# Window attention with its backward pass: the x loads of the loop issued by GpSimd in place of SyncE

## The chip, the cores and the metric

The kernel runs on one core of one Trainium2 chip. A core has a matrix engine (TensorE, PE in the profile; its weight loads are listed apart as PEld), a vector engine (VectorE, DVE), a scalar engine (ScalarE, ACT), GpSimd (POOL) and SyncE (SP). They run side by side, each with its own stream of instructions, and wait for each other on semaphores. Data moves between main memory (HBM) and the on-chip memory (SBUF) by transfers that sixteen DMA engines carry out; an engine only issues them. In this kernel SyncE and GpSimd issue nearly all of them. Matrix products land in PSUM, eight banks that VectorE and ScalarE read out.

The metric is the device time in microseconds (us). The kernel before takes 2007.22 us, the median of three runs (1998.82, 2007.22 and 2007.71).

## What is computed

The operation is attention inside windows of 8 by 8 tokens over an image of 256 by 256 tokens with 384 channels, with one head, and its backward pass:

```python
qkv = xw @ wqkv                        # xw: (1024 windows, 64 tokens, 384)
q, k, v = qkv[..., :C], qkv[..., C:2*C], qkv[..., 2*C:]
p = softmax(einsum('bqc,bkc->bqk', q, k) * C ** -0.5)
o = einsum('bqk,bkc->bqc', p, v) @ wo  # out_0, after the windows are put back
# and from grad_out: the gradients of x (out_1), wqkv (out_2) and wo (out_3)
```

All inputs and outputs are bfloat16. `x`, `grad_out`, `out_0` and `out_1` are 50 MB each, so about 102 MB are read from HBM and 102 MB written.

## The kernel before

**Tiling.** A tile holds two windows, that is 128 tokens on 128 partitions. A "quad" is four such tiles, eight windows one below the other, and there are 128 quads. For a quad the kernel holds `xq` (128 tokens by 4 tiles by 384 channels of x), `dq` (the same of `grad_out`), and their transposes `xT` and `dT` with the channels on the partitions. The weights are folded ahead of the loop into four 384 by 384 matrices (`A_sb`, `AT_sb`, `B_sb`, `BT_sb`, lines 84 to 102).

**The software pipeline.** The order of the work is written out by hand: `tc.manual_schedule` (line 359) covers all five engines, so that each engine executes its instructions in the order in which the Python code emits them. One call of `step(c, b, a, ahead)` (lines 315 to 351) works on four quads at once. In step i, quad i+1 is in stage A (its products with `BT_sb` and `A_sb`, function `project`, give `yz`), quad i in stage B (scores `sd`, softmax, the products `uq` and `vq`), quad i-1 in stage C (`attend`, which makes the rows of `out_0` and `out_1`), and quad i+3 is loaded. In between, `filler` (lines 307 to 313) puts pieces of the weight gradient of three finished quads, `gf_group`, into the stream of TensorE: one piece ahead of each half of `attend`, six pieces for three quads.

**The transfers of a step, in the order of each queue.** SyncE issues for step i:

1. `load_turn` (lines 121 to 129): the transposes `dT` and `xT` of quad i+2. They are DMA transposes from SBUF to SBUF.
2. `turn` (line 231): the transpose `PS` of quad i's probabilities and score gradients, which needs the last operation of the softmax (`soft` step 5, line 219).
3. `load` (lines 114 to 119): four loads of `x` for quad i+3.
4. `to_tokens` (line 165): the transpose `tok` of quad i+1's `yz`, which needs the evictions of both projections (lines 161 and 163).

GpSimd issues for step i four loads of `grad_out` for quad i+3 (line 119), then the stores of `attend` for quad i-1: twelve in all, six after each pair of tiles (lines 287 to 292). The stores read from buffers `ob`, eight for each of `o` and `d`.

A queue waits in order: while its next transfer waits for data or for a buffer, those behind it wait too. TensorE reads `dT` in stage A of the next step, `xT` shortly after it, `PS` in stage C of the next step.

**Buffers.** `xq` has 2 * GQ + 4 = 10 buffers, because the weight gradient still reads a quad's `xq` some steps after `attend`. `dq` has 6, `xT` and `tok` 3, `dT`, `yz` and `PS` 2.

**Ahead of the loop** (lines 360 to 363) the first three quads are loaded and two of them transposed.

Of the kernel before, what the change touches and what calls it, by code (L numbers as in the profile page):

```python
# [22 lines left out]
def kernel(  # L23
# [21 lines left out]
    nc = tc.nc  # L45
# [61 lines left out]
    def windows(ap, st, first, count=2):  # L107
        row, col = st["at"]
        return ap[0, row + WIN * first:row + WIN * (first + count), col:col + WIN, :]
# [1 line left out]
    LO, HI = slice(0, WT), slice(WT, P)  # L111
    OTHER = {0: HI, WT: LO}

    def load(st):
        st["xq"] = xq = grp.tile([P, QUAD, C], BF16, tag="xq", name="xq", bufs=2 * GQ + 4)
        st["dq"] = dq = qp.tile([P, QUAD, C], BF16, tag="dq", name="dq", bufs=6)
        for t in range(QUAD):
            nc.sync.dma_start(out=xq[:, t, :], in_=windows(x, st, 2 * t))
            nc.gpsimd.dma_start(out=dq[:, t, :], in_=windows(grad_out, st, 2 * t))  # L119

    def load_turn(st):
        xq, dq = st["xq"], st["dq"]
        st["xT"] = xT = qp.tile([P, QUAD, CK, P], BF16, tag="xT", name="xT", bufs=3)
        st["dT"] = dT = qp.tile([P, QUAD, CK, P], BF16, tag="dT", name="dT")
        for src, dst in ((dq, dT), (xq, xT)):
            k = G_ON_PE if src is dq else 0
            if k < QUAD:
                nc.sync.dma_start_transpose(out=dst[:, k:].rearrange("p t m k -> p (t m) k"),
                                            in_=src[:, k:].rearrange("p t c -> p (t c)"))
# [49 lines left out]
    def over_k(ap, n=P):  # L179
        return ap.unsqueeze(2).broadcast_to([n, QUAD, WT])  # L180

    def soft(st, step):
        sd = st["sd"]
        if step == 0:
# [111 lines left out]
    def gf_group(sts):  # L296
        n = len(sts) * QUAD
        for f in range(2):
            for ma in range(CK):
                pw = ring.tile([P, C], F32, tag="r", name="pg")  # L300
                for i in range(n):
                    st, t = sts[i // QUAD], i % QUAD
                    product(pw[:], st["xq"][:, t, ma * P:(ma + 1) * P], st["UW"[f] + "q"][:, t, :], i == 0, i == n - 1)
                nc.vector.tensor_tensor(out=GF_acc[:, f, ma, :], in0=pw[:], in1=GF_acc[:, f, ma, :], op=ALU.add)  # L304
                yield

    def filler(n):
        while n and fill:
            try:
                next(fill[0])  # L310
                n -= 1
            except StopIteration:
                fill.pop(0)

    def step(c, b, a, ahead):


        def on(st):
            return (lambda f, *r: f(st, *r)) if st is not None else (lambda f, *r: None)
        C_, B, A = on(c), on(b), on(a)  # L320
        B(scores)
        B(soft, 0)
        B(uv, 0, 0)
        B(uv, 0, 1)
        B(soft, 1)
        B(uv, 1, 0)
        B(uv, 1, 1)
        B(soft, 2)
        B(soft, 3)
        B(uv, 2, 0)  # L330
        B(uv, 2, 1)
        for t in range(QUAD):
            A(grad_turn, t)
        B(uv, 3, 0)
        B(uv, 3, 1)
        B(soft, 4)
        for mo in range(CK):
            A(project, 0, mo)
        B(soft, 5)
        B(turn)  # L340
        if ahead is not None:
            load(ahead)
        filler(1)
        C_(attend, (0, 1))
        split[0] = True
        for mo in range(CK):
            A(project, 1, mo)
        A(to_tokens)
        filler(1)
        split[0] = ALL  # L350
        C_(attend, (2, 3))
# [4 lines left out]
    sts = [{"at": q, "i": i} for i, q in enumerate(quads)]  # L356
    n = len(sts)
    AHEAD = 3
    with tc.manual_schedule(engines=MANUAL):
        for i in range(min(AHEAD, n)):  # L360
            load(sts[i])
            if i < AHEAD - 1:
                load_turn(sts[i])
        held = []
        get = lambda i: sts[i] if 0 <= i < n else None
        for i in range(-1, n + 1):
            if AHEAD - 1 <= i + AHEAD - 1 < n:
                load_turn(sts[i + AHEAD - 1])
            step(get(i - 1), get(i), get(i + 1), get(i + AHEAD) if i >= 0 else None)
            if i > 0:  # L370
                held.append(sts[i - 1])
                sts[i - 1] = None
            if held and (len(held) == GQ or i == n):
                fill.append(gf_group(held))
                held = []
        split[0] = False
        filler(1 << 30)
# [62 lines left out]
```

## Time and profile before

| | |
|---|---|
| time, median of three runs | 2007.22 us |
| time of the profiled run | 1999.63 us |
| span of the profile | 1997.5 us |
| ScalarE busy | 1405.4 us (70%) |
| VectorE busy | 1317.2 us (66%) |
| GpSimd busy, nearly all of it issuing | 1122.9 us (56%) |
| moved by the DMA engines | 425.62 MB, mean 213 GB/s |
| loads of `x`: issuer, count, size, median time to landing | SyncE, 512, 96 KB, 4.0 us |
| loads of `grad_out` | GpSimd, 512, 96 KB, 3.9 us |
| transposes `dT`, `xT`, `tok`, `PS`: issuer, count of each, median time to landing | SyncE, 128, 6.4, 6.7, 8.4 and 4.6 us |

The first line of the page gives busy time, share of the span and number of instructions for each engine. SyncE is not in it, because an instruction that issues a transfer counts as busy on GpSimd alone; what SyncE does is read from the timeline of its queue (marked SPq). A line of the timeline has a start and a length in microseconds, the engine, the line of the kernel, the operation, the tile written and the tile read, the number of instructions merged into the line, and in brackets how long the engine stood idle before and what released it. "Landing" is the time from issue until the data is known to have arrived. A line of the waits reads "who waited <- for whom: us in total, times, longest".

### The profile page before, as it was taken

Reading aid. Unit: us, or ns where it says so; the run is one execution under the profiler, and the core shown is the slowest. Engines: PE = TensorE matmul, PEld = TensorE weight load, DVE = VectorE, ACT = ScalarE, POOL = GpSimd, SP = SyncE. Lnnn points to the kernel's source line nnn. Section 1 sums busy time; section 2 is a strip of 40 time slices with the busy share of each in tenths; the row PEclk is TensorE's granted clock in tenths of the full one; section 3 lists DMA queues with packets and bytes.
Section 4 is the critical chain, followed back from the end, with each engine's and each line's share of the span. In section 5 each row is a group of like instructions: output and inputs, shape, how many; then the busy total and the mean of one; then the engine's idle time right before and its main releaser. Section 6 shows DMA issues by size and latency. Waiting matters only on the chain. (4 is left out here: it accounts for less than half of the span.)

```text
span 1997.5 us, 52374 instructions
## 1 busy us (share of the span) xinstructions
PE 1967.7 (99%) x19418; PEld 1192.8 (60%) x19418; DVE 1317.2 (66%) x2979; ACT 1405.4 (70%) x3213; POOL 1122.9 (56%) x2054
## 2 busy tenths in 40 slices
PE   8899999999999999999999999999999999999998
PEld 4456656665666666566566656666665566566655
DVE  5666666666666666666666666666666666666666
ACT  5776767677777767777776777677776777776773
POOL 3555555565555556555655555565555556555643
PEclk9999999999999999999999999999999999999999
DMA  9999999999999999999999999999999999999993
GB/s 201 211 217 223 208 213 215 224 215 221 216 218 223 210 213 223 219 219 208 227 210 223 219 211 213 223 223 215 215 214 214 212 217 213 223 211 222 217 206 96
DMA packets 1042272, 425.62 MB, mean 213 GB/s; under 512 B 925792, under 2 KB 1016672, under 8 KB 1042016
## 3 DMA queue, kind: packets, MB, share of 16 engines
q1 hardware_dynamic: 943312, 270.60, 81.2%
q0 software_dynamic: 98304, 151.39, 31.1%
q8 instruction: 152, 2.49, 0.6%
q14 instruction: 104, 0.85, 0.1%
q10 hardware_dynamic: 400, 0.29, 0.0%
HBM read 101.84 MB, written 101.84 MB: 102 GB/s over the span
## 5 line engine op out<-in xcount | busy, mean ns | idle before, releaser
L292 POOL DMA_DIRECT2D out_dram<-o x256 | 139.2, 544 | 707.4 <-ACT o L264 697.4
L264 ACT CAST o<-po 128x384 bf16<-128x384 f32 x512 | 220.4, 482 | 370.0 <-PE pu L253 355.2
L304 DVE TENSOR_TENSOR GF_acc<-pg,GF_acc 128x384 f32<-128x384 f32 x258 | 144.0, 558 | 495.0 <-PE pg L145 343.8
L147 PEld LDWEIGHTS <-xT 128*128 128x128 bf16 x3072 | 291.8, 98 | 182.1
L147 PE MATMUL pj<-B_sb,xT 128*128 128x384 bf16 x1536 | 333.4, 326 | 0.0
L147 PE MATMUL pj<-AT_sb,xT 128*128 128x384 bf16 x1536 | 333.3, 326 | 0.0
L119 POOL DMA_DIRECT2D dq<-in_grad_out_dram x512 | 274.1, 547 | 66.0 <-DMA out_dram<-o 37.7
L147 PE MATMUL pj<-dT,BT_sb 128*128 128x512 bf16 x1152 | 269.7, 379 | 8.8 <-DMA dT<-dq 7.3
L145 PE MATMUL pj<-xT,A_sb 128*64 128x512 bf16 x2304 | 273.0, 380 | 1.6 <-DMA xT<-xq 1.6
L229 ACT CAST uq<-pj 128x384 bf16<-128x384 f32 x512 | 247.6, 484 | 30.6 <-PE pj L147 27.1
L229 ACT CAST vq<-pj 128x384 bf16<-128x384 f32 x512 | 249.9, 488 | 2.4 <-ACT uq L229 0.3
L145 PEld LDWEIGHTS <-xq 128*64 128x64 bf16 x3000 | 210.6, 110 | 46.3
L264 ACT CAST d<-pd 128x384 bf16<-128x384 f32 x512 | 225.2, 503 | 0.4 <-ACT o L264 0.2
L147 PEld LDWEIGHTS <-xq 128*128 128x128 bf16 x1572 | 153.6, 98 | 114.9 <-issue 0.3
L207 ACT COPY ps<-Pb 64x256 bf16<-64x256 bf16 x256 | 103.3, 403 | 149.6 <-DVE Pb L204 148.1
L163 ACT CAST yz<-pj 128x512 bf16<-128x512 f32 x384 | 206.3, 630 | 2.1 <-PE pj L145 1.8
L161 ACT CAST yz<-pj 128x512 bf16<-128x512 f32 x384 | 206.4, 639 | 1.1 <-ACT vq L229 0.7
L145 PEld LDWEIGHTS <-A_sb 128*64 128x64 bf16 x2304 | 155.7, 109 | 84.9 <-DMA xT<-xq 2.0
L147 PEld LDWEIGHTS <-BT_sb 128*128 128x128 bf16 x1152 | 111.5, 98 | 133.9 <-DMA dT<-dq 13.6
L147 PE MATMUL pg<-Uq,xq 128*128 128x384 bf16 x1032 | 181.6, 326 | 0.0
L258 PE MATMUL pd<-tok,ps 128*64 128x384 bf16 x1024 | 181.2, 344 | 0.0
L253 PE MATMUL pu<-xq,PS 64*64 64x384 bf16 x1024 | 174.9, 335 | 4.5 <-DMA PS<-ps 4.3
(67 smaller groups left out, 3382.2 us busy)
## 6 DMA issues: line engine op xcount, KB each, us to landing
xq<-in_x_dram SPq DMA_DIRECT2D x512, 96.0 KB, 4.0
dq<-in_grad_out_dram POOLq DMA_DIRECT2D x512, 96.0 KB, 3.9
out_dram<-o POOLq DMA_DIRECT2D x256, 96.0 KB, 4.2
out_dram<-o POOLq DMA_DIRECT2D x512, 48.0 KB, 4.4
out_dram<-d POOLq DMA_DIRECT2D x256, 96.0 KB, 4.4
out_dram<-d POOLq DMA_DIRECT2D x512, 48.0 KB, 4.4
dT<-dq SPq DMA_TRANSPOSE x128, 6.4
xT<-xq SPq DMA_TRANSPOSE x128, 6.7
```

Of the source, the lines that this page charges most:

```text
L119: nc.gpsimd.dma_start(out=dq[:, t, :], in_=windows(grad_out, st, 2 * t))
L145: nc.tensor.matmul(out[h], lhsT=lhsT[:, h], rhs=rhs, start=start, stop=stop)
L147: nc.tensor.matmul(out, lhsT=lhsT, rhs=rhs, start=start, stop=stop)
L161: ENG[EV["z"][mo]](out=yz[:, mo, :, 0:4:3, :], in_=pj[:])
L163: ENG[EV["y"][mo]](out=yz[:, mo, :, 1:3, :], in_=pj[:])
L207: nc.scalar.copy(out=ps[h, :, w, :], in_=Pb[h, :, :])
L229: cp(out=dst[:, t, :], in_=pj[:])
L253: nc.tensor.matmul(at[o, :], lhsT=turned(st, lhs, t, h), rhs=st[rhs][h, t, :], **{"start": True, "stop": True, **fl})
L258: nc.tensor.matmul(pd[outer if w == 0 else 1 - outer][o, :], lhsT=st["ps"][:, t, w, :], rhs=st["tok"][:, :, t, w, :], **flags)
L264: nc.scalar.copy(out=sb[:], in_=src[outer][:])
L292: nc.gpsimd.dma_start(out=windows(dst, st, 2 * t0 + 1), in_=sb[:])
L304: nc.vector.tensor_tensor(out=GF_acc[:, f, ma, :], in0=pw[:], in1=GF_acc[:, f, ma, :], op=ALU.add)
```

## The change

The loads of `x` inside the loop move from SyncE's queue to GpSimd's, where each stands just ahead of the matching load of `grad_out`. The three quads that are loaded ahead of the loop keep SyncE. The aim is to take issue work from the queue that also issues every transpose. Nothing else changes: the same transfers, sizes, buffers and computations.

```diff
-    def load(st):
+    def load(st, queue):
         st["xq"] = xq = grp.tile([P, QUAD, C], BF16, tag="xq", name="xq", bufs=2 * GQ + 4)
         st["dq"] = dq = qp.tile([P, QUAD, C], BF16, tag="dq", name="dq", bufs=6)
         for t in range(QUAD):
-            nc.sync.dma_start(out=xq[:, t, :], in_=windows(x, st, 2 * t))
+            queue.dma_start(out=xq[:, t, :], in_=windows(x, st, 2 * t))
             nc.gpsimd.dma_start(out=dq[:, t, :], in_=windows(grad_out, st, 2 * t))
...
         if ahead is not None:
-            load(ahead)
+            load(ahead, nc.gpsimd)
...
         for i in range(min(AHEAD, n)):
-            load(sts[i])
+            load(sts[i], nc.sync)
```

## The prediction

> **What bounds the kernel now.** I read the busy times first, then the busy times by stretch, then who waits for whom on TensorE, then one step of the two issuing queues in order of time, then the durations and landings of the transfers.
>
> ```profile
> PE 1967.7 (99%) x19418; PEld 1192.8 (60%) x19418; DVE 1317.2 (66%) x2979; ACT 1405.4 (70%) x3213; POOL 1122.9 (56%) x2054
> ```
>
> TensorE is busy 99% of the span at full granted clock. Nothing else can lengthen the time except by making TensorE wait, and an edit that adds no work to TensorE can win no more than the time in which it waits now. The stretches say how much that is (columns: window, its length, then busy microseconds of PE, PEld, DVE, ACT, POOL, clock, DMA share, GB/s):
>
> ```profile
> 60.00:80.00 20.00, 14.81 (x135) 7.76 (x132) 12.11 (x30) 14.22 (x32) 11.90 (x22) 1.00 1.13 202
> 80.00:100.00 20.00, 18.67 (x169) 10.94 (x170) 12.00 (x28) 13.44 (x32) 9.97 (x19) 1.00 1.17 204
> ...
> 640.00:840.00 200.00, 200.00 (x2001) 121.79 (x1997) 133.43 (x302) 142.13 (x327) 114.03 (x209) 1.00 1.16 217
> ```
>
> From 640 to 840 us TensorE never rests, but between 60 and 100 us it rests for 5.2 + 1.3 = 6.5 us. Over the loop from 40 to 1940 us the same view adds up to 1885.8 of 1900 us: 14.2 us of rest, 9.4 of them before 240 us. What ended the rests is in the waits of PE (us, times, longest):
>
> ```profile
> PE pj L147 <- DMA dT<-dq: 7.3, 6, 2.4
> ...
> PE pu L253 <- DMA PS<-ps: 4.3, 5, 1.6
> ...
> PE pj L145 <- DMA xT<-xq: 1.6, 1, 1.6
> ```
>
> All three are transposes issued by SyncE, in its program order. One step of SyncE's queue (start, length, what; a step of TensorE, from one group of score products to the next, is 1007.55 to 1022.75 = 15.20 us):
>
> ```profile
> 1002.95 1.46 SPq L128 DMA_TRANSPOSE dT<-dq  x1
> 1004.58 3.60 SPq L128 DMA_TRANSPOSE xT<-xq  x1
> 1008.35 1.20 SPq L233 DMA_TRANSPOSE PS<-ps  x1
> 1009.59 2.79 SPq L118 DMA_DIRECT2D xq<-in_x_dram  x4
> 1012.49 5.45 SPq L167 DMA_TRANSPOSE tok<-yz  x1
> 1018.16 1.45 SPq L128 DMA_TRANSPOSE dT<-dq  x1
> ```
>
> SyncE issues back to back: 1.46 + 3.60 + 1.20 + 2.79 + 5.45 = 14.50 of 15.21 us, the rest in gaps of 0.2 us. It is late, too. `PS` of a step can go when the last subtraction into `ps` ends, 7.6 us into the step (1015.15); it is issued at 1023.18, 8 us later. So SyncE is a second bottleneck that just keeps up, and TensorE stalls when it slips. The slack of `dT`: issued at 1018.16, it lands a median 6.4 us later (1024.6) and is read at 1012.16 + 15.20 = 1027.36. That leaves 2.8 us, while its slowest landing is 10.4 us.
>
> **What the Trainium skill says.** "DMA: Bandwidth & Descriptors", section "Issuing engines are not separate DMA queues": transfers of all issuers run on the same 16 DMA engines; another issuer saves only the time its sequencer needs to issue. That is this edit, and here the saving lands on a saturated sequencer. The same page, "SWDGE vs HWDGE vs iDMA": GpSimd writes its descriptors in software into SBUF, which VectorE can lock it out of; the trace shows no such loss (512 gradient loads at 518 to 680 ns each beside a VectorE at 66%). The same page, "Queues, rings and completion order": each DMA engine takes turns between the queues, packet by packet; no view here isolates that, but it is why I expect `x` packets on GpSimd's queue to slow the transposes about as they do now. "Perfetto Trace Analysis", section "DMA Instruction — SWDGE (GPSIMD)": the recorded time of a GpSimd DMA ends with its descriptors, not with the data; the rows agree (547 ns against 3.9 us to landing).
>
> **The change, part by part.**
>
> *Removed from SyncE:* 125 of its 128 groups of four `x` loads, at the mean of this row (min/median/max ns):
>
> ```profile
> L118 SPq DMA_DIRECT2D xq<-in_x_dram x512: 575/600/2127, 1.2 to 1927.9; - x171
> ```
>
> Four medians are 2.4 us, in the step above 2.79 us. SyncE's step falls from 14.5 to about 11.8 us, so it gains some 3 us a step until a wait holds it. That wait is `tok`, which needs the last `yz` eviction (ends at 1005.04, 12.7 us into its step). Issued there, `tok` ends 17.5 us in, that is 2.3 us into the next step; `dT` follows at 2.4 instead of 10.6, lands at about 8.8, and is needed at 4.6 + 15.2 = 19.8: slack 11 us for 2.8. `PS` goes at 7.6, lands 4.6 us later at 12.2 and is read 8.6 us into the next step, at 23.8: slack 11.6 us. Both exceed the excess of the slowest landing over the median (10.4 - 6.4 = 4.0 us). So the transpose waits in the loop should go.
>
> *Added to GpSimd:* four issues a step, placed between the gradient loads it already issues:
>
> ```profile
> 1010.68 0.56 POOL L290 DMA_DIRECT2D out_dram<-d  x1
> 1011.23 2.15 POOL L119 DMA_DIRECT2D dq<-in_grad_out_dram  x4
> 1017.92 0.55 POOL L292 DMA_DIRECT2D out_dram<-o  x1 [4.54 <-ACT o L264]
> ```
>
> 4 x 0.55 = 2.2 us more; it stands idle for 4.54 us right behind these loads, waiting for the next result, so the issue time fits. A step holds 16 issues now, 20 then: 20 x 0.55 = 11.0 of 15.2 us. The stores queued behind may slip by a microsecond or two; their buffers (eight for `o`, eight for `d`, four of each a step) give two steps, 30 us, before ScalarE waits. Cost on the path: nothing.
>
> *Added wait one:* a slot of `xq` must be free. The load of quad i+3 takes the slot of quad i-7, whose last reader is the second filler of the step before; that group's add into GF_acc starts at 1006.37, the gradient loads at 1011.23. Free 4.9 us ahead: no wait, though `x` is now asked for 13.6 us earlier than SyncE asks (1024.84 against 1011.23).
>
> *Added wait two:* GpSimd's issues wait for their own earlier transfers. The third gradient load at 526.71 waited 1.34 us for a store issued at 520.97, eight issues before; so eight can be under way.
>
> ```profile
> POOL dq L119 <- DMA out_dram<-o: 37.7, 47, 2.1
> ```
>
> A burst of six stores and eight loads will meet this more often. Twenty issues, eight at a time, at a landing of 4.4 us need 20 / 8 x 4.4 = 11.0 us, again under 15.2. The break-even landing is 15.2 x 8 / 20 = 6.1 us. This is the unknown: I take 4.4 to 5.5 us, since the bytes stay the same; the high end of the range covers more.
>
> *DMA engines:* the same 96 KB transfers land in 4.0 us from SyncE and 3.9 us from GpSimd; I cost the change of queue at nothing.
>
> *Start:* with empty buffers GpSimd runs ahead and issues two groups of `x` 20 and 35 us before SyncE did, eight loads of 96 KB = 786 KB, at the mean 213 GB/s 3.7 us of transfer, beside SyncE's first transposes. Between 0 and 3.7 us; I take 1.5. Against it SyncE loses `x` groups at 35.55, 50.16 and 66.42 us, just ahead of the stalls.
>
> Sum: 1999.6 us is the time of the profiled run. Of the 14.2 us of rest I let 12 go, and add 1.5 for the start: 1999.6 - 12.0 + 1.5 = 1989.
>
> **The rivals.**
>
> *Nothing is gained.* SyncE's issue is slow because the DMA engines are full (ten tenths in nearly every slice, `xT` from 1.4 us up to 5.1): GpSimd's denser bursts take that share away, transposes get as long as the saving, and the stalls stay. For it: transposes cost SyncE more than their minimum (`dT` 1.41 us least, 2.25 median). Against it: total bytes are the same, and SyncE could lose 3 us a step before being as late as now. Time: as before, 2000 to 2007; I say 2003.
>
> *Slower: GpSimd becomes the bound.* If the burst lifts the mean landing of GpSimd's transfers over 6.1 us, its queue lags, stores keep their buffers, ScalarE waits, PSUM banks stay full, TensorE stalls. At 6.2 us a step takes 20 / 8 x 6.2 = 15.5 us: 0.3 x 127 steps = 38 us, so 2045; each further 0.1 us costs 32 us. For it: landings from GpSimd already reach 11 us. Against it: 4.4 is the median now, and half the burst is bytes that were in flight anyway.
>
> **How the numbers follow.** Stalls go: 0.64, 1989. Nothing gained: 0.19, 2003. GpSimd bound: 0.17, 2045. The three runs of before lie from 1998.8 to 2007.7, with nothing in the page to say why; if those 8 us are something other than the stalls, the likeliest case reaches 1997. The lowest I can argue is all rest gone and no cost at the start, 1999.6 - 14.2 = 1985, less what the 1% of rest outside that stretch may give. I set 1979 to 2027: below it little, above it the greater part of the slow case. Faster by 0.5% means under 1997.2, slower over 2017.3: 0.65, 0.19, 0.16.
>
> **What would show it.** Right: `dT` issued 2 to 3 us into the step, its waits gone from PE's list, SyncE idle ahead of `tok`, GpSimd near 1400 us of busy time, the stretch from 60 to 100 us nearly full. Wrong: GpSimd's waits for its own loads in the hundreds of microseconds, a wait of ScalarE's `o` or `d` copies for stores, or transposes longer by 3 us a step.

## The result: 12.7% slower, and the profile after

The changed kernel takes 2260.16 us (median of four runs, 2250.03 to 2266.77) against 2005.01 us for the kernel before on the same chip: a ratio of 1.1273, 95% interval 1.1222 to 1.1325. The forecast was 1989 us in a range up to 2027 us. The time went the other way.

The first line of the page after the change, busy time and share of the span by engine:

```profile
PE 2039.9 (90%) x19418; PEld 1194.0 (53%) x19418; DVE 1317.7 (58%) x2979; ACT 1417.6 (63%) x3213; POOL 1384.9 (61%) x2554
```

The span grew by 2264.7 - 1997.5 = 267.2 us. TensorE's busy time grew by 72.2 us for the same 19418 matmuls, and its rest from 29.8 to 224.8 us, by 195.0. GpSimd got its 500 issues more (262 us, near the 1400 us foreseen). The three stretches of before, in the changed kernel (busy microseconds of PE, PEld, DVE, ACT, POOL, then clock, DMA share, GB/s):

```profile
60.00:80.00 20.00, 16.67 (x135) 8.23 (x134) 12.18 (x30) 14.25 (x32) 13.12 (x24) 0.91 1.17 214
80.00:100.00 20.00, 20.00 (x192) 11.76 (x192) 12.88 (x30) 14.12 (x34) 14.53 (x27) 1.00 1.24 234
640.00:840.00 200.00, 177.68 (x1727) 104.60 (x1723) 114.70 (x260) 122.85 (x280) 123.65 (x228) 0.97 1.13 187
```

The start is better, as foreseen: between 60 and 100 us TensorE rests 3.3 us in place of 6.5. The steady loop, which had no rest at all, now loses 22 of 200 us. Who TensorE waits for, over the whole run (us, times, longest):

```profile
PE pu L253 <- DMA PS<-ps: 113.6, 73, 3.8
PE pj L147 <- DMA dT<-dq: 83.3, 54, 4.1
```

`dT` and `PS` led that list before too, with 7.3 and 4.3 us. But SyncE is no longer the one that keeps them. Its queue, over one step:

```profile
1001.65 6.21 SPq L167 DMA_TRANSPOSE tok<-yz  x1
1011.53 1.49 SPq L128 DMA_TRANSPOSE dT<-dq  x1
1013.18 2.92 SPq L128 DMA_TRANSPOSE xT<-xq  x1
1016.29 1.93 SPq L233 DMA_TRANSPOSE PS<-ps  x1
1018.32 6.28 SPq L167 DMA_TRANSPOSE tok<-yz  x1
```

After `tok` (ended at 1007.86) SyncE stands idle until 1011.53. In the list of its waits one entry leads, `dT`'s line L128 that waits for the gradient loads:

```profile
SPq L128 <- DMA dq<-in_grad_out_dram: 435.8, 123, 7.9
```

For 118 of the 125 quads that the loop loads, `dT` starts less than 0.3 us after the last load of its `dq` lands; before the change, for none. Here that load was issued by GpSimd at 1002.75 and landed at 1011.4. The first gradient load of a quad is issued a median of 20.8 us into its step of TensorE, where it was 3.7: GpSimd is behind by about a step. Its queue around one burst of loads:

```profile
1014.13 0.56 POOL L290 DMA_DIRECT2D out_dram<-d  x1
1014.69 0.55 POOL L118 DMA_DIRECT2D xq<-in_x_dram  x1
...
1017.89 0.54 POOL L118 DMA_DIRECT2D xq<-in_x_dram  x1
1019.93 0.52 POOL L119 DMA_DIRECT2D dq<-in_grad_out_dram  x1 [1.50 <-DMA out_dram<-d]
```

The last gradient load waits 1.50 us for a store; eight issues before it stands the store of 1014.13, which took 5.5 us to land. In no run of this document does GpSimd issue a transfer before the eighth one ahead of it has landed, and its transfers signal eight semaphores in turn; these are the eight "places" of what follows. Over the whole run the waits of GpSimd have changed their kind. First the leading line of the kernel before, then lines of the changed one:

```profile
POOL out_dram L292 <- ACT o L264: 697.4, 239, 28.2
```

```profile
POOL out_dram L292 <- DMA xq<-in_x_dram: 89.9, 46, 5.4
POOL out_dram L289 <- DMA dq<-in_grad_out_dram: 72.5, 34, 4.7
...
POOL out_dram L292 <- ACT o L264: 42.4, 16, 21.1
```

Before, GpSimd waited for ScalarE's results, so that it seemed to have time to spare. After, it waits for its own transfers, and hardly ever for results. I counted the pauses of over 0.1 us ahead of its transfers. One is put down to its own queue if it ended within 0.6 us after the landing of the eighth transfer before: 102 us before, 740 us after. Pauses that ended in the same way with ScalarE's copy of the data to be stored: 700 us before, 24 us after. With the 1385 us of issuing, the waits for its own queue fill 94% of GpSimd's span (61% before). Why each transfer holds its place so long is in the landings (KB each, median us from issue to landing), 3.9 to 4.4 us before:

```profile
dq<-in_grad_out_dram POOLq DMA_DIRECT2D x512, 96.0 KB, 5.9
xq<-in_x_dram POOLq DMA_DIRECT2D x500, 96.0 KB, 5.7
out_dram<-o POOLq DMA_DIRECT2D x256, 96.0 KB, 6.7
```

So the chain is: GpSimd's queue, the last gradient load, `dT` and behind it `PS` on SyncE, TensorE, the results, GpSimd's stores. The rate of the DMA engines in bytes is not what stops it: they moved the same 426 MB at a mean of 188 GB/s, and at 213 before.

### The profile page after: what moved, and what is told of

Its sections match the earlier page's. It is cut to its first block, busy times and chain, and to the rows that moved or that the text cites. A ratio compares the mean times of both kernels' runs of the same rounds, so it can differ in the third digit from the quotient of the medians.

```text
span 2264.7 us, 52492 instructions
## 1 busy us (share of the span) xinstructions
PE 2039.9 (90%) x19418; PEld 1194.0 (53%) x19418; DVE 1317.7 (58%) x2979; ACT 1417.6 (63%) x3213; POOL 1384.9 (61%) x2554
## 5 line engine op out<-in xcount | busy, mean ns | idle before, releaser
L147 PE MATMUL pj<-dT,BT_sb 128*128 128x512 bf16 x1152 | 290.9, 401 | 95.1 <-DMA dT<-dq 83.3
L118 POOL DMA_DIRECT2D xq<-in_x_dram x500 | 272.1, 544 | 57.2 <-DMA out_dram<-o 26.2
L145 PE MATMUL pj<-xT,A_sb 128*64 128x512 bf16 x2304 | 300.7, 409 | 1.5 <-DMA xT<-xq 1.4
L292 POOL DMA_DIRECT2D out_dram<-o x256 | 139.3, 544 | 255.9 <-DMA xq<-in_x_dram 83.7
L289 POOL DMA_DIRECT2D out_dram<-o x256 | 147.2, 575 | 208.2 <-DMA dq<-in_grad_out_dram 72.5
L161 ACT CAST yz<-pj 128x512 bf16<-128x512 f32 x384 | 210.7, 631 | 46.3 <-issue 21.0
L163 ACT CAST yz<-pj 128x512 bf16<-128x512 f32 x384 | 209.6, 626 | 25.6 <-PE pj L145 24.8
L274 DVE CAST Uq<-pu 128x384 bf16<-128x384 f32 x256 | 141.5, 553 | 132.8 <-PE pu L253 131.2
L145 PEld LDWEIGHTS <-A_sb 128*64 128x64 bf16 x2304 | 164.1, 117 | 102.6 <-issue 25.9
```

The source lines that it names most:

```text
L118: queue.dma_start(out=xq[:, t, :], in_=windows(x, st, 2 * t))
L145: nc.tensor.matmul(out[h], lhsT=lhsT[:, h], rhs=rhs, start=start, stop=stop)
L147: nc.tensor.matmul(out, lhsT=lhsT, rhs=rhs, start=start, stop=stop)
L161: ENG[EV["z"][mo]](out=yz[:, mo, :, 0:4:3, :], in_=pj[:])
L163: ENG[EV["y"][mo]](out=yz[:, mo, :, 1:3, :], in_=pj[:])
L274: nc.vector.tensor_copy(out=st["Uq"][:, t0, :], in_=pu[0][:])
```

## The experiments

Three theories were set against each other. **A:** GpSimd's queue is the bound; twenty transfers a step, eight places, each held until its transfer has landed. **B:** the loads are only too late, and more lookahead would cure it. **C:** `x` on GpSimd's queue takes DMA time from the transposes.

The table sums up all kernels. Landing is the mean over all of GpSimd's transfers, from the issue and landing times in the trace; "under way" is their number times that landing over the span (for after 2548 x 6.03 / 2264.7 = 6.8). Ratios are against the kernel before on the same chip; its medians there lie between 2002.98 and 2007.69 us.

| kernel | on GpSimd a step | landing us | under way | time us | ratio (95%) |
|---|---|---|---|---|---|
| before | 16 | 4.48 | 4.6 | 2005.01 | 1 |
| after | 20 | 6.03 | 6.8 | 2260.16 | 1.1273 (1.1222 to 1.1325) |
| e1_swap: x on GpSimd, gradient on SyncE | 16 | 4.55 | 4.7 | 2007.14 | 0.9993 (0.9976 to 1.001) |
| e2_half: two of four x on GpSimd | 18 | 5.17 | 6.0 | 1993.96 | 0.9907 (0.9866 to 0.9947) |
| e7_three: three of four | 19 | 5.55 | 6.6 | 2041.59 | 1.0187 (1.0143 to 1.023) |
| e4_ahead4: loads a step earlier | 20 | 6.09 | 6.8 | 2292.12 | 1.1414 (1.134 to 1.1487) |
| e5_split: x loads in halves | 24 | 4.98 | 6.4 | 2362.37 | 1.1791 (1.1741 to 1.184) |
| e6_notok: leaves out 127 tok transposes | 20 | 3.21 | 4.1 | 1986.12 | 0.9902 (0.9864 to 0.9941) |
| e9_spread: x loads between the stores | 20 | 5.31 | 6.6 | 2057.09 | 1.0252 (1.0195 to 1.0308) |
| e11_stores_sp: two stores on SyncE | 18 | 5.35 | 6.1 | 1994.46 | 0.9963 (0.9947 to 0.998) |
| e3_act: x on ScalarE | 16 | 6.78 | 6.5 | 2143.13 | 1.063 (1.0557 to 1.0702) |
| e12_act_half: two of four x on ScalarE | 16 | 5.11 | 5.2 | 1999.63 | 0.9981 (0.9967 to 0.9995) |
| e10_half_spread: e2, spread | 18 | 5.23 | 6.1 | 1989.19 | 0.9927 (0.9908 to 0.9945) |

Every kernel with 6.4 or more under way is slower than before, every one with 6.1 or less is not. That mark, found after the runs, tells a full queue from one with room; it does not measure the loss. The mean stays under eight although GpSimd's transfers land in the order of their issue in every run: in the changed kernel all eight are under way for 40% of the time and seven for 33%, and after a landing that it waited for, GpSimd takes a median of 0.55 us to start the next transfer. Issuing and waiting for its own queue fill 94 to 95% of GpSimd's span in after, e4, e5, e7 and e9, 86% in e3, and at most 82% in all others.

### Is it x on GpSimd, or the number? (e1_swap, e11_stores_sp)

```diff
-            nc.gpsimd.dma_start(out=dq[:, t, :], in_=windows(grad_out, st, 2 * t))
+            (nc.sync if queue is nc.gpsimd else nc.gpsimd).dma_start(out=dq[:, t, :], in_=...)
```

> The x loads of the loop stay on GpSimd, but the gradient loads go to SyncE in their place: GpSimd issues 16 transfers a step as before the change, SyncE four loads a step as before. Theory A (GpSimd is the bound, because its 20 transfers a step go eight at a time and each takes 6.0 us to land): back near before, 2000 to 2020 us, mean landing of GpSimd's transfers near 4.5 us. Theory B (nothing is wrong with the number; the x load placed beside the gradient load reaches the transposes too late): GpSimd's part is as after, x no later, so dT still waits for a load; 2020 to 2100 us. Theory C (x on GpSimd's queue, in larger packets, slows the transposes): x is still on that queue but the bytes per queue are those of before; 2005 us.

The time is that of before, the landing too: all of `x` on GpSimd costs nothing as long as the gradient leaves. B falls in its first form. C foresaw 2005 us here too, so this run does not part it from A.

```diff
-                nc.gpsimd.dma_start(out=windows(dst, st, 2 * t0 + 1), in_=sb[:])
+                (nc.sync if t0 == 0 else nc.gpsimd).dma_start(out=windows(dst, st, 2 * t0 + 1), in_=sb[:])
```

> As after the change (all four x loads of a step on GpSimd beside the gradient loads), but the two whole-tile stores of the first half of attend go to SyncE: 18 transfers a step on GpSimd, six on SyncE. Theory A (the number on GpSimd counts, whatever is in it): as with half of the x loads, 1985 to 2020 us. If it is x on GpSimd that hurts: over 2100 us. If SyncE's added wait for attend's results holds up its transposes: 2020 to 2100 us, with tok issued later than 13 us into its step.

This is the changed kernel with two of its twenty issues moved, and the whole loss of 255 us is gone. SyncE had room for the two stores between `PS` and `tok`: `tok` is issued at a median of 12.7 us into TensorE's step. What counts is the load on GpSimd's queue, not whose data it is.

### Where is the threshold? (e2_half, e7_three)

```diff
-            queue.dma_start(out=xq[:, t, :], in_=windows(x, st, 2 * t))
+            (queue if t < 2 else nc.sync).dma_start(out=xq[:, t, :], in_=windows(x, st, 2 * t))
```

(`t < 3` in e7_three.)

> Of the four x loads of a step, two go to GpSimd and two stay on SyncE: 18 transfers a step on GpSimd. Theory A: a threshold; at a landing of about 5.2 us, 18 / 8 x 5.2 = 11.7 us a step leaves GpSimd under 15.2 us, so 1990 to 2040 us. Theory C: a dose, about half of the loss, 2100 to 2150 us. Theory B: dT and xT wait for the latest load, which is still GpSimd's: over 2100 us.

> Three of the four x loads of a step on GpSimd, one on SyncE: 19 transfers. Eighteen took 1994 us and left GpSimd 247 us of waits for its own transfers and 409 us for data; twenty took 2260. Theory A: near the threshold, the spare 409 us of waiting for data is used up by one more transfer and longer landings: 1995 to 2080 us. Theory C as a dose: halfway, 2100 to 2150 us.

Eighteen are 0.9% faster than sixteen, nineteen 1.9% slower, twenty 12.7% slower: a threshold, not a dose. e2_half also shows SyncE's side of the prediction on its own. One step of its SyncE queue:

```profile
1003.46 4.77 SPq L167 DMA_TRANSPOSE tok<-yz  x1
1008.39 2.85 SPq L128 DMA_TRANSPOSE dT<-dq  x1
1011.42 3.42 SPq L128 DMA_TRANSPOSE xT<-xq  x1
1015.00 1.78 SPq L233 DMA_TRANSPOSE PS<-ps  x1
1016.82 1.23 SPq L118 DMA_DIRECT2D xq<-in_x_dram  x2
1018.66 4.74 SPq L167 DMA_TRANSPOSE tok<-yz  x1
```

`tok` is issued 15.20 us apart, held only by its data, and there is a pause of 0.6 us ahead of the second. `dT` is issued at a median of 2.7 us into TensorE's step, where it was 11.0. With two `x` loads fewer, SyncE has the slack that it lacked. TensorE's rest falls from 29.8 to 23.0 us.

### Is it lookahead? (e4_ahead4)

```diff
     AHEAD = 3
+    LOAD = 4
...
-        for i in range(min(AHEAD, n)):
+        for i in range(min(LOAD, n)):
...
-            step(get(i - 1), get(i), get(i + 1), get(i + AHEAD) if i >= 0 else None)
+            step(get(i - 1), get(i), get(i + 1), get(i + LOAD) if i >= 0 else None)
```

(and 11 buffers for `xq`, 7 for `dq`.)

> As after the change, but each quad is loaded one step earlier (four quads ahead in place of three, one more buffer each for xq and dq; the transposes stay where they are). It gives every load a step, 15 us, more slack. Theory A (a bound on the rate of GpSimd's transfers): the rate is the same, so only the one-time slack is won, 2235 to 2265 us. Theory B (loads are late): the slack cures it, 1990 to 2020 us. Theory C: no change, 2260 us.

B falls: a step more of lookahead makes it no faster (even slower than A allows, by 27 us; why is open). The wait only moves. TensorE's leading wait in this kernel is for ScalarE, and ScalarE waits for the stores that have to free its buffers:

```profile
PE pj L145 <- ACT o L264: 149.4, 88, 4.7
ACT o L264 <- DMA out_dram<-o: 279.7, 152, 5.8
```

The loads come early enough for TensorE now (its waits for `dT` and `PS` are 2.5 and 2.3 us), but the stores behind them do not, and the results pile up. That is the mark of a bound on rate.

### Is it the count or the bytes? (e5_split)

```diff
-                queue.dma_start(out=xq[:, t, :], in_=windows(x, st, 2 * t))
+                queue.dma_start(out=xq[LO, t, :], in_=windows(x, st, 2 * t, 1))
+                queue.dma_start(out=xq[HI, t, :], in_=windows(x, st, 2 * t + 1, 1))
```

> As after the change, but each x load of the loop is issued as two halves of 48 KB (64 partitions each): 24 transfers a step on GpSimd, the same bytes. Theory A (eight transfers at a time, each held for its landing): the halves of stores land about as late as whole ones (5.2 to 5.4 against 5.0 to 6.7 us), so the step grows with the count, 24 / 20 of 17.4 us = 20.9 us or, with landings a little shorter, 19.5: 2500 to 2650 us. Theory C (GpSimd's queue gets a fixed share of the DMA engines, in bytes): unchanged, 2240 to 2290 us.

In between. With the same bytes, four transfers more cost 102 us, so the count matters; but the landing fell by 17%, so a fifth more transfers cost only 4.5% more time. A with a fixed landing is too simple: how long a place is held depends on the traffic. The run does not isolate the places either: GpSimd's issuing grew from 1385 to 1678 us, while its waits for its own queue fell from 740 to 553 us.

### What makes the landings long? (e6_notok, e9_spread, e3_act, e12_act_half)

```diff
+        if st["i"] > 0:
+            st["tok"] = first[0]
+            return
```

> As after the change, but tok is transposed for the first quad only and read again for all others (leaves out 127 of the 128 tok transposes, 24 of the 52 blocks of 128 x 128 that SyncE transposes a step): 20 transfers a step on GpSimd as after. It asks what makes the landings long. If they wait for the transposes on the shared DMA engines (theory A with theory C as its cause): landing falls from 6.0 us to 4 to 5 us, GpSimd fits its 20 transfers, 1975 to 2000 us. If the landing is long because GpSimd's own queue is deep: no change in the landing, 2200 to 2265 us.

All twenty transfers on GpSimd, and 1986 us. (The kernel computes a false gradient of `x`; it serves for the landings alone.) The landings in this kernel:

```profile
xq<-in_x_dram POOLq DMA_DIRECT2D x500, 96.0 KB, 2.3
out_dram<-o POOLq DMA_DIRECT2D x256, 96.0 KB, 3.5
```

Without 24 of the 52 transposed blocks the mean landing falls from 6.03 to 3.21 us: the transposes lengthen the landings. How much of the fall is their own, and how much comes of a queue that is no longer full, this run does not part. It is C's resource, but it acts through A's eight places.

```diff
-            load(ahead, nc.gpsimd)
+            load(ahead, None)          # the gradient only
...
         C_(attend, (0, 1))
+        if ahead is not None:
+            load_x(ahead)              # four x loads, GpSimd
```

> As after the change, but GpSimd issues the four x loads between the two halves of attend's stores, where before the change it stood idle, and not beside the gradient loads: 20 transfers, in two smaller bursts. If only the mean rate counts (theory A in its plain form: 20 transfers at 6.0 us, eight at a time): no change, 2230 to 2270 us. If the burst of six stores and eight loads is what fills the eight places and lengthens the landings: the landing stays near 5.2 us and the time falls to 1990 to 2060 us.

Four fifths of the loss is gone (2057 in place of 2260 us) with the same twenty transfers: with the eight loads in one burst the landings are 6.0 us, without it 5.3. A in its plain form did not foresee that. Why the burst does it was not taken further. It also means that e2_half and e11_stores_sp, which take two transfers out of the burst, do not by themselves tell number from burst. e9_spread beside e11_stores_sp does in part: at nearly the same landing (5.31 and 5.35 us) twenty transfers lose 2.5% and eighteen nothing.

```diff
-            load(ahead, nc.gpsimd)
+            load(ahead, nc.scalar)
```

> The x loads of the loop are issued by ScalarE: GpSimd as before the change, SyncE relieved as after it. It measures the saving on SyncE that the prediction counted, without the load on GpSimd. Theories A and C: no loss from GpSimd; the transpose waits of TensorE go, against that ScalarE issues four loads of about 0.6 us, 2.4 us a step, in its own order at 70% busy: 1985 to 2010 us; above 2010 if ScalarE's evictions come late by it. Theory B has no view on it.

Every theory missed this one. GpSimd has only its sixteen transfers, SyncE has lost its `x` loads, and still it takes 6.3% longer. The landings of this kernel:

```profile
xq<-in_x_dram ACTq DMA_DIRECT2D x500, 96.0 KB, 7.0
out_dram<-o POOLq DMA_DIRECT2D x256, 96.0 KB, 6.8
...
dT<-dq SPq DMA_TRANSPOSE x128, 9.5
xT<-xq SPq DMA_TRANSPOSE x128, 11.2
```

All transfers of all queues land later (`dT` 6.4 us, `xT` 6.7 us before), and the issue of a transpose holds SyncE longer: `xT` a median of 4.7 us in place of 3.0. GpSimd's queue holds 6.5 transfers, but it is not what keeps the transposes here. `dT` follows the last landing of its `dq` by a median of 5.4 us, and SyncE issues back to back again, now with transposes alone:

```profile
1003.10 2.76 SPq L128 DMA_TRANSPOSE dT<-dq  x1
1006.03 5.79 SPq L128 DMA_TRANSPOSE xT<-xq  x1
1011.99 2.10 SPq L233 DMA_TRANSPOSE PS<-ps  x1
1014.19 5.77 SPq L167 DMA_TRANSPOSE tok<-yz  x1
1020.18 4.69 SPq L128 DMA_TRANSPOSE dT<-dq  x1
```

The mean durations of its four transposes add up to 14.9 us a step, 11.6 before; with the gaps of some 0.2 us between them that is more than the 15.2 us of a step. So SyncE is the bound again, and its saving went into longer transposes. The prediction's first rival expected that of GpSimd's queue.

> Two of the four x loads of a step on ScalarE's queue, two on SyncE; GpSimd as before the change. All four on ScalarE made every transfer land later (6.8 us on GpSimd) and took 2143 us. If a third queue with work takes its turns from the transposes whenever it has any (theory C in its queue form): half the dose, 2050 to 2090 us. If four loads at once were too many beside the stores and two are not: 1990 to 2005 us, as with two on GpSimd.

Its edit is that of e2_half with ScalarE in place of GpSimd. Two loads are borne, at no gain worth the name (0.9981); half the dose, 2050 to 2090 us, did not come. Whether four on ScalarE hurt because a third queue takes its turns from the transposes, or because of the moment at which ScalarE issues them, these two runs do not tell apart.

### A version that beats both (e10_half_spread, e2_again)

e10_half_spread is e2_half with its two GpSimd loads issued between the two halves of `attend`'s stores, as in e9_spread.

> Two of the four x loads of a step on GpSimd, issued between the two halves of attend's stores in place of beside the gradient loads; the other two stay on SyncE: 18 transfers on GpSimd in smaller bursts. Spreading shortened the landings at 20 transfers (5.3 against 6.0 us), so theory A with bursts expects a landing of about 5 us and a time as with 18 transfers in one burst or a little less: 1985 to 1995 us. If the placement beside the gradient loads does not matter below the threshold: 1994 us.

> The kernel with two of the four x loads of a step on GpSimd and two on SyncE once more, in five rounds on the chip of its rivals, as the version that beats before and after: 1990 to 1996 us, a ratio of 0.99 to before.

Side by side: 1989.19 us (0.9927, 0.9908 to 0.9945) and 1993.18 us (0.9946, 0.9928 to 0.9965). They beat before by 0.7% and 0.5%. The intervals overlap, though every run of e10_half_spread (up to 1989.81 us) is below every run of e2_again (from 1991.46). 1989 us is what the prediction promised for the full change, and TensorE's rest in e10_half_spread, 18.3 us for 29.8, is the promised gain of some 12 us.

## Why the prediction was wrong, point by point

**SyncE as the second bottleneck, and what its relief is worth: right, but not reached in the changed kernel.** e2_half and e10_half_spread give `dT` at the foreseen place (2.7 and 2.5 us into the step) and 1994 and 1989 us. In the changed kernel SyncE had the same slack and lost it waiting for GpSimd's loads: its pauses ahead of `dT` add up to 523 us. e3_act shows that the relief also hangs on where the loads go.

**"The issue time fits": right, and beside the point.** Twenty issues of 0.55 us are 11 of 15.2 us. A queue is not bound by its issue time if each issue must first get a place.

**"Added wait two" is the step that failed.** The sum was 20 / 8 x 4.4 = 11.0 us with a break-even landing of 6.1 us. The mechanism was named, and both of its factors were mis-sized, in the same direction. The landing does not stay at 4.4 to 5.5 us "since the bytes stay the same": its mean rose from 4.48 to 6.03 us. That alone gives 20 / 8 x 6.03 = 15.1 us, just short of a loss. And the eight places are not all full in the mean: the changed kernel has 6.8 under way, with which the break-even is 15.2 x 6.8 / 20 = 5.2 us and not 6.1. A step took 17.3 us from one group of score products to the next. (20 / 6.8 x 6.03 = 17.7 us is no separate check on that, because 6.8 was worked out from the same landing and the span.) A sign was in the profile of before: at sixteen transfers GpSimd already waited 102 us for its own.

**"The change of queue at nothing": wrong.** The prediction compared the landings of the two queues as they stood, 4.0 and 3.9 us, with only half of the loads on each. e3_act (the same sixteen transfers, 6.78 us for 4.48) and e6_notok (the same twenty, 3.21 for 6.03) show that a queue's landing depends on what else is asked of the DMA engines.

**"The stores may slip by a microsecond or two": wrong by the same step.** Stores and loads share one in-order queue that cannot keep up, so the slip adds up until the lookahead is used: a quad's gradient loads go out some 17 us later in their step.

**The slot of `xq`: right.** The waits of the `x` loads for TensorE, which reads the old contents of a slot, come to about 4 us in the whole run.

**The start: right in sign.** 60 to 100 us rests half as much. The 1.5 us for the early transfers was not measured apart.

**The rivals.** "GpSimd becomes the bound" was the right mechanism at a chance of 0.17, in the right words: stores late, landing over the break-even. It was sized at 2045 us because it, too, divided by eight, and foresaw a landing just over the break-even. That nothing is gained because the transposes take longer was wrong as a cause here, though `tok` did go from 4.8 to 6.2 us; it is what happened in e3_act.

**What no step had: a wait costs more than itself.** The prediction took TensorE's waits for the whole of what could be lost. Some 63 of the 267 us are TensorE at half clock after waits; see the last section.

The Trainium skill's sentence that another issuer saves only issue time ("DMA: Bandwidth & Descriptors", section "Issuing engines are not separate DMA queues") held for SyncE. I took it to say that nothing else changes. The runs show what else changes with the issuer: how full its eight places are, its landings, and what is stuck behind what. No run gave GpSimd more than eight places, so whether that would lift the bound is not shown.

## What to carry to other kernels

Before moving a transfer to another queue, count the load of that queue as number a step times landing, against the places it really fills (here 6.4 to 6.8 of eight), and take the landing under the new load: at 4.6 under way there was no room for four more in one burst, though the engine was idle 44% of the time. The list of its waits tells whether an issuing engine waits for results or for its own transfers, but it does not tell how much more fits: before the change 700 us of GpSimd's pauses were for results, and two more transfers a step fitted while four did not. Move a part first: the threshold is sharp, and eighteen transfers a step won 0.4 to 0.9% where twenty lost 12.7%.

## What the runs showed of the hardware that I had not expected

TensorE's clock falls after a wait. The changed kernel at the wait of 3.45 us that ends at 1024.06, and then the stretches around it (the clock is the third number from the end):

```profile
1024.06 0.35 PE L253 MATMUL pu<-xq,PS 64*64 64x384 bf16 x1 [3.45 <-DMA PS<-ps]
...
1024.25 0.48 PE L253 MATMUL pw<-dq,Pb 64*64 64x384 bf16 x1
```

```profile
1024.00:1028.00 4.00, 3.94 (x32) 1.74 (x34) 1.95 (x4) 2.23 (x5) 1.19 (x3) 0.57 1.31 235
1028.00:1032.00 4.00, 4.00 (x54) 2.29 (x51) 1.24 (x3) 1.60 (x4) 2.56 (x5) 1.00 0.90 112
```

For some 3.4 us the clock is half, and a matmul that takes a median of 0.32 us before the change takes 0.48 to 0.53. The trace has 35 such stretches, together 126.6 us, 34 of them at a wait of 1.8 to 4.1 us; at half clock they lose about 63 us, most of the 72 us by which TensorE's busy time grew. The kernel before has one, at its very end. The Trainium skill, "TensorE: Matmul & The Clock Gate", section "Part 1: The HAM clock gate (the "warmup" mystery)", tells of half clock after an idle window of about 3.4 us and of 3.4 us until it is full again. The length agrees; here waits from 1.8 us upward sufficed, though not every such wait did. The trace shows what tells them apart. All 35 stretches begin on one grid of 3.413 us, to within 0.02 us. In the grid window just ahead of each of the 34, TensorE was busy for at most 49% of the time. After the first 10 us of the kernel, every window under 41% was followed by a drop, and none over 49% was; in the loop of the kernel before, none was under 50%. By these figures a wait costs clock when it empties more than about half of one such window; spread over two windows, the same wait can cost no more than itself. (Busy times of the matmuls are modelled; e4_ahead4 and e5_split have one drop each after a busier window, 67% and 53%.)

The other surprise is e3_act: with all `x` loads on a third queue, the same transfers landed later on every queue. With half of them there (e12_act_half) GpSimd's mean landing was 5.11 us, for 4.48 before and 6.78 in e3_act. The cause is open.
